# Rewriting a fused attention and Mish kernel: Mish as one ScalarE function from PSUM, k and q exponentials in the projection stage, attention combine beside the up-projection

## The chip, the core and the metric

The kernel runs on one core of one Trainium2 chip. The metric is the device time of one execution in microseconds (us); the profile's span of the same execution is about 2 us shorter. Before the change the median was 227.62 us over four runs (three of them 226.75 to 227.79, one slow at 241.48). Engines are named as the profile names them: PE is TensorE, PEld its weight loads, DVE VectorE, ACT ScalarE, POOL GpSimd, SP SyncE.

## The reference

Two branches read the same layer-normalised input of 2048 rows and 448 columns, and their results are added to the input.

```python
xn = _layernorm(x)                                  # x: (1, 2048, 448), bf16
# branch A: linear attention, 16 heads of 28 columns
q, k, v = split(xn @ wqkv)
pq, pk  = q @ w_phi, k @ w_phi                      # per head, 28 x 28
phi_q = concat([softmax(pq), softmax(-pq)])         # phi_k the same from pk
kv = einsum("bhsf,bhsd->bhfd", phi_k, v);  z = phi_k.sum(s)
o  = (phi_q @ kv) / (phi_q @ z + 1e-6)
A  = o.reshape(B, S, D) @ wo
# branch B: feed-forward, 448 -> 1792 -> 448, with Mish
h   = xn @ w1 + b1
B   = (h * tanh(log(1 + exp(h)))) @ w2             # written in a stable form there
return x + A + B
```

## The kernel before

Both kernels fold `w_phi` into the q and k weights first. The old kernel then computes Mish in three passes, with a change of ScalarE's function table between them. The parts that matter (cuts are marked `# ...`):

```python
# ScalarE and VectorE, up-projection: h has 56 groups of 512 columns, four PSUM banks in turn
for grp in range(NGRP):
    b_exp.inc(act.activation(sp_buf[:, fc, cols], hring[grp % HR], ACT.Exp, bias=b1T[:, fc:fc + 1]))
    # every fourth group on ScalarE, the others on VectorE: h + bias, kept in SBUF
    b_hb.inc(dve.tensor_scalar(hb_all[:, fc, cols], hring[grp % HR], b1T[:, fc:fc + 1], None, op0=ALU.add))
    # ... beside it k: two exponentials per tile on ScalarE, reduce and reciprocal on VectorE, phik on GpSimd

for fc in range(FC):                                             # second pass
    b_ln.inc(act.activation(sp_buf[:, fc, :], sp_buf[:, fc, :], ACT.Ln, bias=1.0))
# ... meanwhile TensorE does v and q, and VectorE copies q, unexponentiated, to SBUF

for k in range(2 * FC):                                          # third pass
    b_tanh.inc(act.activation(t_tmp[k % 2], sp_buf[:, fc, half], ACT.Tanh))
    b_mul.inc(dve.tensor_tensor(actT[:, fc, cols], hb_all[:, fc, cols], t_tmp[k % 2], ALU.mult))

# only then, per row tile: q exponentials, attention numerator and denominator, combine, output
for t in range(-2, NT):
    pe_nd(t + 2); pe_ffn2(t); pe_transposes(t + 1); pe_wo(t)     # TensorE
    # VectorE per tile: copy, two products, sum, reciprocal, product, and the residual
```

The softmax here doesn't subtract the row's maximum and nothing guards it: scores larger than these inputs give would overflow.

Of the kernel before, what the change touches and what calls it, by code (L numbers as in the profile page):

```python
# [6 lines left out]
ALU = mybir.AluOpType  # L7
# [4 lines left out]

# [7 lines left out]
KC = 4  # L20
KP = 112
FC = F // P
TCW = 512
TC = S // TCW
QG = 4
LN_EPS = 1e-5
NGRP = TC * FC
HR = 4
NDW = QG * (DH + 2)


class Ctr:

    def __init__(self, sem, name):
        self.sem = sem
        self.name = name
        self.n = 0

    def inc(self, ins, by=1, expect=None):
        ins.then_inc(self.sem, by)  # L40
        self.n += by
        if expect is not None:
            assert self.n == expect, f"{self.name}: count {self.n} != expected {expect}"
        return self.n


def wait(eng, ctr, val):
    if val > 0:
        assert val <= 30000, (ctr.name, val)
        eng.wait_ge(ctr.sem, val)  # L50
# [6 lines left out]
def bass_parallel_sum__linear_kernel_hedgehog__dense_activation_mish__prompt_kernel(  # L57
    nc, A_x, A_wqkv, A_w_phi, A_wo, B_x, B_w1, B_b1, B_w2, out
):
    es = ExitStack()  # L60
    with es:
        _kernel(es, nc, A_x, A_wqkv, A_w_phi, A_wo, B_w1, B_b1, B_w2, out)


def _kernel(es, nc, A_x, A_wqkv, A_w_phi, A_wo, B_w1, B_b1, B_w2, out):
    def C(name):
        return Ctr(es.enter_context(nc.semaphore(name)), name)

    def sb(name, shape, dtype, side, stack):
        return stack.enter_context(nc.sbuf_tensor(name, shape, dtype, side=side))  # L70

    x2 = A_x[0]
    out2 = out[0]

    PKGRP = [2 + round(i * (NGRP - 4) / (NT - 1)) for i in range(NT)]
    assert len(set(PKGRP)) == NT and PKGRP[-1] < NGRP

    L = es
    ident = sb("ident", [P, P], BF16, "left", L)
    eps_col = sb("eps_col", [P, 1], FP32, "left", L)  # L80
    Wbd = sb("Wbd", [KP, QG, KP], BF16, "left", L)
    b1_rows = sb("b1_rows", [FC, P], BF16, "left", L)
    b1T = sb("b1T", [P, FC], FP32, "left", L)
    KVZ1 = sb("KVZ1", [KP, 2 * QG, QG, DH + 2], BF16, "left", L)
    Wv = sb("Wv", [KP, KC, D], BF16, "left", L)
    Wpq = sb("Wpq", [KP, KC, D], BF16, "left", L)
    Wpk = sb("Wpk", [KP, KC, D], BF16, "left", L)
    xnT = sb("xnT", [KP, KC, S], BF16, "left", L)
    sL_A = ExitStack()
    x_all = sb("x_all", [P, NT, D], BF16, "left", sL_A)  # L90
    stats = [sb(f"stats{i}", [P, 6], FP32, "left", sL_A) for i in range(2)]
    mv = [sb(f"mv{i}", [P, 2], FP32, "left", sL_A) for i in range(2)]
    std = [sb(f"std{i}", [P, 1], FP32, "left", sL_A) for i in range(2)]
    rstd = [sb(f"rstd{i}", [P, 1], FP32, "left", sL_A) for i in range(2)]
    xn_buf = [sb(f"xn{i}", [P, D], BF16, "left", sL_A) for i in range(2)]
    peakA_left = nc.sbuf_base
    sL_A.close()
    hb_all = sb("hbact", [P, FC, S], BF16, "left", L)
    actT = hb_all
    t_tmp = [sb(f"t_tmp{i}", [P, TCW * 2], BF16, "left", L) for i in range(2)]  # L100
    sL_B = ExitStack()
    sp_buf = sb("sp_buf", [P, FC, S], BF16, "left", sL_B)

    sR_phik = ExitStack()
    phik = sb("phik", [P, NT, 2, D], BF16, "right", sR_phik)
    sR_W1 = ExitStack()
    W1 = sb("W1", [KP, KC, F], BF16, "right", sR_W1)
    sR_D1 = ExitStack()
    Ek = [sb(f"Ek{i}", [P, 2, D], BF16, "right", sR_D1) for i in range(2)]
    Sk = [sb(f"Sk{i}", [P, 2 * H], FP32, "right", sR_D1) for i in range(2)]  # L110
    rSk = [sb(f"rSk{i}", [P, 2 * H], FP32, "right", sR_D1) for i in range(2)]
    sR_A = ExitStack()
    Wqk_tmp = sb("Wqk_tmp", [KP, KC, 2 * D], BF16, "right", sR_A)
    WT_sb = [sb(f"WT_sb{i}", [KP, QG, KP], BF16, "right", sR_A) for i in range(2)]
    peakA = nc.sbuf_top - nc.sbuf_base
    sR_A.close()
    sR_D1.close()
    sR_W1.close()
    sR_C = ExitStack()
    v_ext = sb("v_ext", [P, NT, H, DH + 1], BF16, "right", sR_C)  # L120
    pqT_all = sb("pqT_all", [KP, QG, S], BF16, "right", sR_C)
    peakC = nc.sbuf_top - nc.sbuf_base
    sL_B.close()
    W2 = sb("W2", [P, FC, D], BF16, "left", L)
    Wo = sb("Wo", [KP, KC, D], BF16, "left", L)
    NEQ = 3
    NOSB = 3
    sR_E = ExitStack()
    es.enter_context(sR_E)
    EqT = [sb(f"EqT{i}", [KP, 2, QG, P], BF16, "left", sR_E) for i in range(NEQ)]  # L130
    t1 = [sb(f"t1_{i}", [P, H, DH + 1], FP32, "left", sR_E) for i in range(2)]
    t2 = [sb(f"t2_{i}", [P, H, DH + 1], FP32, "left", sR_E) for i in range(2)]
    rden = sb("rden", [P, H], FP32, "left", sR_E)
    Sq = [sb(f"Sq{i}", [P, 2, H], FP32, "left", sR_E) for i in range(2)]
    o_sb = [sb(f"o_sb{i}", [P, D], BF16, "left", sR_E) for i in range(NOSB)]
    oT_sb = [sb(f"oT_sb{i}", [KP, KC, P], BF16, "left", sR_E) for i in range(2)]
    out_sb = [sb(f"out_sb{i}", [P, D], BF16, "left", sR_E) for i in range(2)]
    x_ring2 = [sb(f"x_ring2_{i}", [P, D], BF16, "left", sR_E) for i in range(2)]
    peakE = nc.sbuf_top - nc.sbuf_base
    assert min(peakA, peakC, peakE) >= 0, (peakA, peakC, peakE)  # L140
    del peakA_left

    PB0 = es.enter_context(nc.psum_tensor("PB0", [P, TCW], FP32))
    PB1 = es.enter_context(nc.psum_tensor("PB1", [P, TCW], FP32))
    PBnd = es.enter_context(nc.psum_tensor("PBnd", [P, 2 * TCW], FP32))
    PB4 = es.enter_context(nc.psum_tensor("PB4", [P, TCW], FP32))
    PB5 = es.enter_context(nc.psum_tensor("PB5", [P, TCW], FP32))
    PB6 = es.enter_context(nc.psum_tensor("PB6", [P, TCW], FP32))
    PB7 = es.enter_context(nc.psum_tensor("PB7", [P, TCW], FP32))
    xT_ps = [PB0.bitcast(BF16)[:, 0:KC * P].rearrange("p (c n) -> p c n", c=KC),  # L150
             PB1.bitcast(BF16)[:, 0:KC * P].rearrange("p (c n) -> p c n", c=KC)]
    WT_ps = [PB6.bitcast(BF16)[:, 0:QG * KP].rearrange("p (g n) -> p g n", g=QG),
             PB5.bitcast(BF16)[:, 0:QG * KP].rearrange("p (g n) -> p g n", g=QG)]
    Wp_ps = [PB7[:, 0:D], PB4[:, 0:D]]
    b1T_ps = PB5.bitcast(BF16)[:, 1008:1024]
    hring = [PBnd[:, 0:TCW], PBnd[:, TCW:2 * TCW], PB4[:, :], PB5[:, :]]
    pk_ps = [PB6[:, 0:D], PB7[:, 0:D]]
    vring = [PB0[:, 0:D], PB1[:, 0:D]]
    kv_ps = [PBnd[:, 0:QG * (DH + 1)], PBnd[:, TCW:TCW + QG * (DH + 1)]]
    pqring = [PB4[:, :], PB5[:, :]]  # L160
    out_ps = [PB0[:, 0:D], PB1[:, 0:D], PB5[:, 0:D], PB6[:, 0:D], PB7[:, 0:D]]
    NOUT = len(out_ps)
    NEARLY = NOUT
    nd_ps = PBnd[:, :].rearrange("p (s n) -> p s n", s=2)
    oT_ps = PB4.bitcast(BF16)[:, 0:KC * P].rearrange("p (c n) -> p c n", c=KC)

    ld_x = [C(f"ld_x{i}") for i in range(4)]
    ld_w1 = C("ld_w1")
    ld_b1 = C("ld_b1")
    ld_wphi = C("ld_wphi")  # L170
    ld_wqk = C("ld_wqk")
    ld_wv = C("ld_wv")
    ld_w2a = C("ld_w2a")
    ld_w2b = C("ld_w2b")
    ld_wo = C("ld_wo")
    ld_x2 = [C("ld_x2_0"), C("ld_x2_1")]
    g_init = C("g_init")
    out_dma = [C("o_dma0"), C("o_dma1")]
    a_b1 = C("a_b1")
    a_dve = C("a_dve")  # L180
    a_st = C("a_st")
    a_ag = C("a_ag")
    a_sq = C("a_sq")
    a_rs = C("a_rs")
    a_xn = C("a_xn")
    a_tp = C("a_tp")
    a_cp = C("a_cp")
    a_wtp = C("a_wtp")
    a_wt = C("a_wt")
    a_wpm = C("a_wpm")  # L190
    a_wp = C("a_wp")
    b_pe = C("b_pe")
    b_hb = C("b_hb")
    b_hba = C("b_hba")
    b_exp = C("b_exp")
    d_pe = C("d_pe")
    d_exp = C("d_exp")
    d_red = C("d_red")
    d_rcp = C("d_rcp")
    d_phi = C("d_phi")  # L200
    b_ln = C("b_ln")
    b_tanh = C("b_tanh")
    b_mul = C("b_mul")
    c_pe = C("c_pe")
    c_dve = C("c_dve")
    c_pool = C("c_pool")
    e_pqa = C("e_pqa")
    c_pq = C("c_pq")
    d_kv = C("d_kv")
    d_kvz = C("d_kvz")  # L210
    d_fin = C("d_fin")
    e_expq = C("e_expq")
    e_nd = C("e_nd")
    e_ndrd = C("e_ndrd")
    e_dl = C("e_dl")
    e_o = C("e_o")
    e_tp = C("e_tp")
# [579 lines left out]
```

## Time and profile before

| stage of the old kernel | window, us | what limits it |
|---|---|---|
| layernorm, weight folding | 0 to 32 | a serial chain of VectorE and ScalarE |
| up-projection, k | 32 to 97 | TensorE |
| Ln pass, v, q | 97 to 124 | ScalarE |
| Tanh pass, kv | 124 to 154 | ScalarE |
| first combines | 154 to 178 | VectorE |
| down-projection | 178 to 225 | TensorE |

Lines of the profile page of the kernel before: the span; the busy time of each engine; and two rows in which the span is cut into 40 slices, PE's busy share and the clock granted to it, each in tenths (9 is 90% or more).

```profile
span 225.3 us, 3204 instructions
...
PE 186.9 (83%) x1153; PEld 105.6 (47%) x1153; DVE 166.2 (74%) x319; ACT 157.9 (70%) x244; POOL 41.8 (19%) x43
...
PE   0239869999999999959999862995576899999995
...
PEclk9999999999999999999999995899678599999999
```

PE is 83% busy, yet the digits dip between slices 23 and 32, and the clock dips with them.

The same kernel by stages: the window, then the busy time (and number of instructions) of PE, PEld, DVE, ACT and POOL, then the mean granted clock, the share of the DMA engines and GB/s.

```profile
0.00:32.00 32.00, 15.61 (x121) 13.05 (x121) 20.46 (x71) 15.62 (x38) 7.22 (x17) 1.00 0.55 147
32.00:97.00 65.00, 63.97 (x301) 29.94 (x302) 49.10 (x75) 59.52 (x106) 23.78 (x14) 1.00 0.00 1
97.00:124.00 27.00, 24.94 (x123) 13.87 (x123) 21.30 (x34) 26.97 (x17) 4.61 (x3) 1.00 0.00 1
124.00:154.00 30.00, 22.39 (x196) 13.70 (x193) 20.38 (x30) 29.48 (x38) 6.22 (x9) 0.89 0.25 68
154.00:178.00 24.00, 15.49 (x106) 8.96 (x107) 20.97 (x45) 12.71 (x24) 0.00 (x0) 0.75 0.15 43
178.00:225.30 47.30, 44.48 (x311) 26.07 (x310) 33.97 (x69) 13.55 (x25) 0.00 (x0) 0.98 0.20 57
```

In the third and fourth windows ACT is busy 27 of 27 and 29.5 of 30 us: the Ln and Tanh passes. In the fifth nothing but DVE is near full, PE works 15.5 of 24 us and its clock falls to 0.75. These 81 us are what the change goes after.

Groups of instructions: line, engine, operation, output and inputs, shapes, count, then busy time, mean duration in ns, idle time before.

```profile
L599 ACT ACTIVATE t_tmp<-sp_buf 128x1024 bf16<-128x1024 bf16 x28 | 27.7, 1053 | 0.0
L304 POOL TENSOR_TENSOR phik<-Ek,rSk 128x896 bf16<-128x896 bf16 x16 | 27.2, 1698 | 60.0 <-DVE rSk L681 59.8
...
L584 ACT ACTIVATE sp_buf<-sp_buf 128x2048 bf16<-128x2048 bf16 x14 | 25.3, 1895 | 0.0
...
L571 ACT ACTIVATE sp_buf<-PBnd,b1T 128x512 bf16<-128x512 f32 x28 | 19.0, 702 | 0.7 <-PE PBnd L389 0.4
```

The costs a prediction can start from: 0.70 us for a ScalarE function of 512 columns from PSUM with a bias, 25.3 and 27.7 us for the passes that go away, and 1.70 us for GpSimd's product of 896 columns.

### The profile page before, as it was taken

The numbers are of one execution on the slowest core, as the hardware profiler recorded it, in microseconds if no ns is written. First come the engines' busy times: TensorE is split into PE (matmuls) and PEld (weight loads), VectorE is DVE, ScalarE is ACT, GpSimd is POOL, SyncE is SP. The second block draws the span as 40 slices with busy tenths as digits, with TensorE's granted clock in tenths as the row PEclk, the third lists the DMA queues.
The fourth block names the chain that finished last, engine by engine and source line by source line (L and its number), as shares of the span: only waits on it lengthen the run. The fifth ranks groups of instructions, "written<-read, shape, count | busy, mean of one in ns | idle before, by whom it ended". The sixth has DMA issues, their size and how long they took to land.

```text
span 225.3 us, 3204 instructions
## 1 busy us (share of the span) xinstructions
PE 186.9 (83%) x1153; PEld 105.6 (47%) x1153; DVE 166.2 (74%) x319; ACT 157.9 (70%) x244; POOL 41.8 (19%) x43
## 2 busy tenths in 40 slices
PE   0239869999999999959999862995576899999995
PEld 0138744444444444425555751442443556566552
DVE  2539973578887878969878567775999997887831
ACT  2126876999999999899999999998355224335120
POOL 8220000053545344661000019000000000000000
PEclk9999999999999999999999995899678599999999
DMA  6968000000000000000000009301012221221211
GB/s 198 258 161 214 1 3 1 0 0 3 0 0 0 0 3 0 1 1 3 0 0 0 3 0 299 61 0 41 0 41 63 64 81 41 64 62 41 75 50 41
DMA packets 9710, 10.54 MB, mean 47 GB/s; under 512 B 832, under 2 KB 9232, under 8 KB 9696
## 3 DMA queue, kind: packets, MB, share of 16 engines
q1 hardware_dynamic: 9008, 7.51, 11.6%
q0 software_dynamic: 688, 2.84, 5.2%
q8 instruction: 9, 0.15, 0.3%
q14 instruction: 5, 0.04, 0.1%
HBM read 8.52 MB, written 1.84 MB: 46 GB/s over the span
## 4 chain that ended last, share of the span: by engine, by line
PE 50%; ACT 27%; DVE 13%; DMA 4%; issue 3%; POOL 2%; POOLq 0%; DVEq 0%; ACTq 0%
PE PB L484 13%; ACT t_tmp L599 11%; PE PBnd L389 11%; ACT sp_buf L584 11%; PE PB L389 11%; PE PB L371 5%; PE PB L503 4%; DMA Wqk_tmp<-in_A_wqkv_dram 4%; DVE stats L650 2%; PE PBnd L474 2%; PE PB L494 1%; POOL Wbd L289 1%; DVE WT_sb L658 1%; ACT std L526 1%; DVE o_sb L752 1%
## 5 line engine op out<-in xcount | busy, mean ns | idle before, releaser
L304 POOL TENSOR_TENSOR phik<-Ek,rSk 128x896 bf16<-128x896 bf16 x16 | 27.2, 1698 | 60.0 <-DVE rSk L681 59.8
L623 ACT ACTIVATE oT_sb<-PB 112x512 bf16<-112x512 bf16 x16 | 9.6, 598 | 38.3 <-PE PB L494 38.3
L484 PE MATMUL PB<-W,hbact 128*128 128x448 bf16 x154 | 31.4, 356 | 0.0
L695 DVE TENSOR_SCALAR hbact<-PBnd,b1T 128x512 bf16<-128x512 f32 x28 | 19.8, 727 | 14.5 <-ACT sp_buf L571 14.4
L389 PE MATMUL PBnd<-xnT,W 112*128 112x512 bf16 x112 | 28.6, 395 | 0.0
L599 ACT ACTIVATE t_tmp<-sp_buf 128x1024 bf16<-128x1024 bf16 x28 | 27.7, 1053 | 0.0
L389 PE MATMUL PB<-xnT,W 112*128 112x512 bf16 x112 | 27.1, 379 | 0.0
L725 DVE TENSOR_TENSOR hbact<-hbact,t_tmp 128x1024 bf16<-128x1024 bf16 x28 | 19.7, 703 | 9.4 <-ACT t_tmp L599 9.3
L584 ACT ACTIVATE sp_buf<-sp_buf 128x2048 bf16<-128x2048 bf16 x14 | 25.3, 1895 | 0.0
L571 ACT ACTIVATE sp_buf<-PB,b1T 128x512 bf16<-128x512 f32 x28 | 19.2, 694 | 3.2 <-PE PB L389 2.9
L462 PE MATMUL PB<-W,hbact 128*128 128x448 bf16 x70 | 15.1, 376 | 7.0 <-DMA W<-in_B_w_dram 6.0
L484 PEld LDWEIGHTS PB<-W,hbact 128*128 128x128 bf16 x154 | 14.9, 99 | 12.8 <-issue 0.4
L571 ACT ACTIVATE sp_buf<-PBnd,b1T 128x512 bf16<-128x512 f32 x28 | 19.0, 702 | 0.7 <-PE PBnd L389 0.4
L389 PEld LDWEIGHTS PBnd<-xnT,W 112*128 112x128 bf16 x112 | 11.3, 101 | 13.5 <-issue 1.7
L678 DVE TENSOR_REDUCE Sk<-Ek 128x32 f32<-128x896 bf16 x16 | 17.2, 1075 | 0.4 <-ACT Ek L557 0.4
L389 PEld LDWEIGHTS PB<-xnT,W 112*128 112x128 bf16 x112 | 11.0, 98 | 12.9 <-issue 0.3
L430 PE MATMUL PB<-xnT,Wpq 112*112 112x512 bf16 x64 | 16.4, 379 | 0.7 <-ACT hbact L574 0.7
L503 PE MATMUL PB<-Wo,oT_sb 112*128 112x448 bf16 x64 | 17.0, 394 | 0.0
L417 PE MATMUL PB<-Wv,xnT 112*128 112x448 bf16 x64 | 14.7, 353 | 2.1 <-DVE v_ext L708 2.1
L371 PE MATMUL PB<-Wpk,xnT 112*128 112x448 bf16 x64 | 14.7, 352 | 0.0
L474 PE MATMUL PBnd<-KVZ,EqT 112*128 112x120 bf16 x128 | 10.9, 238 | 4.0 <-DVE t_0 L743 2.4
L462 PEld LDWEIGHTS PB<-W,hbact 128*128 128x128 bf16 x70 | 7.0, 103 | 14.8 <-issue 7.9
(72 smaller groups left out, 306.3 us busy)
## 6 DMA issues: line engine op xcount, KB each, us to landing
x_all<-in_A_x_dram SPq DMA_DIRECT2D x4, 448.0 KB, 5.8
out_dram<-out_sb SPq DMA_DIRECT2D x16, 112.0 KB, 1.7
W<-in_B_w_dram POOLq DMA_DIRECT2D x1, 1568.0 KB, 8.8
W<-in_B_w_dram SPq DMA_DIRECT2D x2, 784.0 KB, 6.2
x_ring_0<-in_A_x_dram SPq DMA_DIRECT2D x8, 112.0 KB, 2.1
x_ring_1<-in_A_x_dram SPq DMA_DIRECT2D x8, 112.0 KB, 2.1
Wqk_tmp<-in_A_wqkv_dram POOLq DMA_DIRECT2D x1, 784.0 KB, 8.1
Wv<-in_A_wqkv_dram POOLq DMA_DIRECT2D x1, 392.0 KB, 9.3
```

Source lines behind the costliest of these rows:

```text
L304: d_phi.inc(gp.tensor_tensor(dst, src_, rs, ALU.mult), expect=t + 1)
L371: ins = pe.matmul(pk_ps[j], xnT[:, c, t * P:(t + 1) * P], Wpk[:, c, :], start=(c == 0), stop=(c == KC - 1))
L389: ins = pe.matmul(hring[grp % HR], W1[:, c, fc * P:(fc + 1) * P], xnT[:, c, tc * TCW:(tc + 1) * TCW], start=(c == 0), stop=(c == KC - 1))
L462: pe.matmul(out_ps[t % NOUT], actT[:, fc, t * P:(t + 1) * P], W2[:, fc, :], start=(fc == 0), stop=False)
L484: pe.matmul(out_ps[j], actT[:, fc, t * P:(t + 1) * P], W2[:, fc, :], start=(fc == 0), stop=False)
L503: ins = pe.matmul(out_ps[j], oT_sb[t % 2][:, c, :], Wo[:, c, :], start=False, stop=(c == KC - 1))
L571: b_exp.inc(act.activation(sp_buf[:, fc, tc * TCW:(tc + 1) * TCW], hring[grp % HR], ACT.Exp, bias=b1T[:, fc:fc + 1]), expect=grp + 1)
L584: b_ln.inc(act.activation(sp_buf[:, fc, :], sp_buf[:, fc, :], ACT.Ln, bias=1.0), expect=fc + 1)
L599: b_tanh.inc(act.activation(t_tmp[k % 2][:, :], sp_buf[:, fc, half * 1024:(half + 1) * 1024], ACT.Tanh), expect=k + 1)
L678: d_red.inc(dve.tensor_reduce(Sk[j][:, :], Ek[j][:, :, :].rearrange("p s (h f) -> p (s h) f", f=DH), AX.X, ALU.add), expect=t + 1)
L695: b_hb.inc(dve.tensor_scalar(hb_all[:, fc, tc * TCW:(tc + 1) * TCW], hring[grp % HR], b1T[:, fc:fc + 1], None, op0=ALU.add), expect=n_hb_d ...
L725: b_mul.inc(dve.tensor_tensor(actT[:, fc, cols], hb_all[:, fc, cols], t_tmp[k % 2][:, :], ALU.mult), expect=k + 1)
```

## The change

The intent: one ScalarE function (Mish) straight from PSUM in place of Exp, Ln and Tanh; the k and q exponentials straight from the projections' PSUM banks, before the up-projection; the attention combine hidden beside the up-projection's matmuls. The program is now recorded as a list of operations, from which the waits are derived. The diff rewrites nearly every line, so it is cut here to its core; names follow the new kernel.

```diff
-    b_ln.inc(act.activation(sp_buf[:, fc, :], sp_buf[:, fc, :], ACT.Ln, bias=1.0))
-    b_tanh.inc(act.activation(t_tmp[k % 2][:, :], sp_buf[:, fc, ...], ACT.Tanh))
-    b_mul.inc(dve.tensor_tensor(actT[:, fc, cols], hb_all[:, fc, cols], t_tmp[k % 2][:, :], ALU.mult))
+    # up-projection group n: 1024 columns, two banks
+    act(lambda a: a.activation(hm[tcp][:, fc, :], PS[:, b:b + 2, :], ACT.Mish, bias=b1T[:, fc:fc + 1]), ...)
 ...
-    a_sq.inc(act.activation(std[j][:, :], mv[j][:, 1:2], ACT.Sqrt, bias=eps_col[:]))
-    a_rs.inc(dve.reciprocal(rstd[j][:, :], std[j][:, :]))
-    a_xn.inc(dve.tensor_scalar(xn_buf[j], x_all[:, t, :], mv[j][:, 0:1], rstd[j], op0=ALU.subtract, op1=ALU.mult))
+    def ln_rstd(t, n):                       # 1/std on GpSimd: add eps, then power -0.5
+        pool(lambda g: g.tensor_scalar(rstd[:, t:t + n], ..., LN_EPS, None, op0=ALU.add), ...)
+        pool(lambda g: g.tensor_tensor(rstd[:, t:t + n], rstd[:, t:t + n], mhalf[:, 0:n], ALU.pow), ...)
+    def ln_norm(t, eng):
+        eng(lambda v: v.tensor_scalar(xn[t % NXN], x_all[:, t, :], mv[:, t, 0:1], rstd[:, t:t + 1],
+                                      op0=ALU.subtract, op1=ALU.mult), ...)
 ...
+    def kexp(j):                             # a pair of row tiles; Ek has two buffers
+        for s in range(2):
+            act(lambda a, s=s: a.activation(Ek[j % 2][:, :, s, :], PS[:, 4:6, 0:D], ACT.Exp,
+                                            scale=(1.0 if s == 0 else -1.0)), ...)
+    def knorm(j):
+        b = j % 2
+        dve(lambda v: v.tensor_reduce(Sk[b], Ek[b], AX.X, ALU.add), ...)
+        dve(lambda v: v.reciprocal(rSk[b], Sk[b]), ...)
+        pool(lambda g: g.tensor_tensor(phik[:, 2 * j:2 * j + 2, :], Ek[b], rSk[b] (broadcast), ALU.mult), ...)
 ...
+    ln(0, dve); ...; ln(1, dve); ln(2, pool)
+    for j in range(NP):                      # eight pairs of row tiles
+        vproj(j)
+        kproj(j); kexp(j)
+        if j + 1 < NP: xT(j + 1)             # x transposes and their copy to SBUF
+        if j >= 1: qproj(...); qexp(...)
+        if j + 3 < NP: ln(j + 3, pool)       # normalisation on GpSimd
+        if j == 2: masks()                   # on GpSimd
+        if j >= 1: knorm(j - 1)
+    qproj(3, 1); qexp(3, 1); knorm(NP - 1)
+    for n in range(2 * FC):                  # up-projection
+        ffn1(n)
+        if n == 5: kvz()
+        if 0 <= n - 6 < NT: nd(n - 6)        # attention and combine of one row tile
+        if 0 <= n - 9 < NT: oTr(n - 9)
+    for t in range(NT): final(t)             # down- and output projection, residual
```

## The prediction

> **What bounds it now.** Span 225.3 us (227.79 timed). The chain of waits is 50% TensorE, 27% ScalarE, 13% VectorE; the limit changes by stage (engine busy time by windows, timeline):
> - 0-32 us, layernorm and weight folding: a serial VectorE/ScalarE chain of 1.2-1.5 us per row tile.
> - 32-97: up-projection and k, TensorE (64.0 of 65 busy).
> - 97-124: the Ln pass on ScalarE (14 x 1.9 us), v and q matmuls beside it.
> - 124-154: the Tanh pass on ScalarE (29.5 of 30).
> - 154-178: attention combine, a VectorE chain near 3.3 us per tile; TensorE 15.5 of 24, clock 0.75.
> - 178-225: down-projection, TensorE: 3.6-4.05 us per tile, of which 14x0.19+4x0.19 = 3.4 is matmul.
>
> **Necessary TensorE work at full clock**, from spacing in the trace (512 columns 0.216 us, 448 columns 0.19, 120 columns 0.073, kv 0.056): up-projection 48.4, q 13.8, v and k 24.3, kv 7.2, combine 9.3, down 42.6, output projection 12.2, transposes 10-15: about 170 us. Some 55 us are waits and cold clock.
>
> **What changes.** Removed: Exp on h (28+28 x 0.70 us), Identity, bias adds on VectorE (42 x 0.72), Ln 25.3, Tanh 27.7, product 19.7, q evacuation 11.0, sixteen Sqrt. Added: 28 Mish of 1024 columns from PSUM. [...] One table load (1.28 us) between Exp and Mish. Combine shrinks to about 2.0 us of VectorE per tile, beside matmuls.
>
> **Sum of the new stages** (estimates):
> 1. Head, to the first dense projection: 12-13 us (weight folding waits for GpSimd's small loads).
> 2. Projections, eight pairs of tiles. Work per pair: TensorE 5.5, VectorE 5.3 (reduce 2.0, reciprocal 0.55, v copy 1.1, statistics 1.5), GpSimd 5.5-6 (phik 3.4, from 1.70 at half size), ScalarE 4.5. Not the work but a cycle binds: k exponential 1.7 -> x transpose copy 1.0 -> v matmuls 1.6 -> v copy 1.2 -> statistics 1.5 -> reduce/reciprocal 2.6 -> phik 3.5 -> k exponential two pairs later: 13.1, so 6.6 us per pair while statistics run, 5.8 after. First pair 9. Ends near 67.
> 3. Up-projection with kv and combine: 48.4+7.2+16x0.93 = 70.5, TensorE-bound; the two combine banks are freed about 2.1 us after they fill, just what TensorE needs to return: 1-2 us of stalls. Ends near 139.
> 4. Down-projection 16 x 3.42 = 54.7: ends near 194; tail 2.8.
>
> Span 195-197; **time 197 us**, 8 in 10 between **187 and 208**. Faster by over 2%: 0.97; within 2%: 0.02; slower: 0.01. About 54 us of Ln and Tanh passes and 20 us of combine stage leave the critical path; about 40 us of that return as TensorE work moved beside them or projections slower than pure matmul time.
>
> **Right if:** two table loads; Mish near 1.13 us each, spaced 1.9-2.8 us by TensorE; up-projection stage 71-75 us at TensorE above 93% busy, clock near 1; down-projection tiles near 3.45 us; projection pairs near 6.6 then 5.8 us with the k exponential waiting for GpSimd.
>
> **Wrong if:** [...]GpSimd's normalisation or power is slow, so projection pairs take 8 us (+12); the projection stage leaves the clock low (+5 to 10); combine banks stall TensorE 1 us per group (+16); or projections run at TensorE's 5.5 us (-8).

The sum came to: the head and the projections to 67 us, the up-projection to 139, the down-projection to 194, the tail 2.8, together 195 to 197 us of span. No term of it is cut: in the stage with Mish it counts TensorE's matmuls alone. What is cut is the working of Mish's 1.13 us, which did not come from a trace, and one clause under "Wrong if". An estimate from the trace of the kernel before comes to nearly the same: 0.70 us for 512 columns from PSUM (L571), plus 512 more at 0.82 ns each (1.053 us for 1024 columns, L599, and 1.895 for 2048, L584), is 1.12 us, under the 1.73 us that a group's eight matmuls take (L389).

## The result, and the profile after

The median was **212.08 us** (210.47 to 212.95, four runs). The ratio to the kernel before is 0.9335, with a 95% interval of 0.9276 to 0.9394. The change is faster, as forecast, but by 15 us instead of 31; the time lies above the range of 187 to 208.

The same lines of the page for the kernel after, with GpSimd's row added:

```profile
span 210.4 us, 2756 instructions
...
PE 181.3 (86%) x1153; PEld 98.0 (47%) x1153; DVE 83.3 (40%) x160; ACT 84.5 (40%) x94; POOL 76.6 (36%) x70
...
PE   0587689395894896899999999999999999999994
...
POOL 8366449999996329200033333442000000000000
PEclk9999699887899797999999999999999999999999
```

The dip has moved. It is now deepest between slices 8 and 16, and POOL's row shows 9 from slice 7 to slice 12.

By stages:

```profile
0.00:23.70 23.70, 11.76 (x96) 8.61 (x97) 7.70 (x21) 10.93 (x12) 15.55 (x25) 0.99 0.98 267
23.70:85.70 62.00, 48.86 (x236) 24.79 (x235) 32.63 (x40) 33.23 (x37) 45.94 (x29) 0.87 0.03 7
85.70:153.00 67.30, 66.20 (x539) 36.70 (x537) 32.98 (x83) 39.20 (x45) 15.09 (x16) 1.00 0.01 1
153.00:210.40 57.40, 54.54 (x288) 27.96 (x286) 10.00 (x16) 1.11 (x1) 0.00 (x0) 1.00 0.10 33
```

The border at 85.7 us is the start of the table load before the first Mish. TensorE's first up-projection matmul starts earlier, at 83.55, and its first down-projection matmul at 152.81. So the last two stages went as predicted or better: the up-projection with all combines inside it took 67.3 us from the table load, or 69.3 from its first matmul (predicted 71 to 72), and the down-projection and tail 57.4 us (54.7 + 2.8). Everything before the first up-projection matmul takes 83.55 us where the prediction had 67. In the second window PE works 48.9 of 62 us at a clock of 0.87, and no engine is full: POOL, the busiest after PE, shows 45.9.

Groups of the kernel after:

```profile
L430 ACT ACTIVATE hm<-PS,b1T 128x1024 bf16<-128x1024 f32 x28 | 31.2, 1114 | 28.2 <-PE PS L420 28.1
L338 POOL TENSOR_TENSOR hm<-hm,rSk 128x1792 bf16<-128x1792 bf16 x8 | 25.7, 3217 | 9.3 <-DVE rSk L337 9.2
L263 POOL TENSOR_SCALAR xn<-x_all,mv,rstd 128x448 bf16<-128x448 bf16 x12 | 22.3, 1867 | 0.6
...
L263 DVE TENSOR_SCALAR xn<-x_all,mv,rstd 128x448 bf16<-128x448 bf16 x4 | 1.4, 393 | 2.3 <-POOL rstd L259 2.3
```

Mish takes 1.114 us; the estimate was 1.13. But the last two lines are the same operation, same shape, on two engines: 0.39 us on DVE, **1.87 us on POOL**. The prediction had put about 0.85 us per tile into its 5.5 to 6 us of GpSimd work: half of the 1.70 us that the product of 896 columns took in the old kernel.

One pair in the timeline (start, duration, engine, line, operation; in brackets the engine's idle time just before and what ended it):

```profile
47.20 0.24 POOL L257 TENSOR_SCALAR rstd<-mv 128x2 f32<-128x2 f32 x1
47.27 1.73 ACT L330 ACTIVATE hm<-PS 128x896 bf16<-128x896 f32 x2 [5.48 <-POOL hm L338]
...
47.52 0.72 POOL L259 TENSOR_TENSOR rstd<-rstd,mhalf 128x2 f32<-128x2 f32 x1
48.35 3.72 POOL L263 TENSOR_SCALAR xn<-x_all,mv,rstd 128x448 bf16<-128x448 bf16 x2
48.88 1.03 ACT L301 ACTIVATE xnT<-PS 112x1024 bf16<-112x1024 bf16 x1
...
49.97 2.79 PE L310 MATMUL PS<-Wqkv,xnT 112*128 112x448 bf16 x8 [2.88 <-ACT xnT L301]
...
52.04 3.21 POOL L338 TENSOR_TENSOR hm<-hm,rSk 128x1792 bf16<-128x1792 bf16 x1
...
55.26 0.23 POOL L257 TENSOR_SCALAR rstd<-mv 128x2 f32<-128x2 f32 x1
55.28 0.92 ACT L330 ACTIVATE hm<-PS 128x896 bf16<-128x896 f32 x1 [3.54 <-POOL hm L338]
```

POOL does not pause: 1/std, two normalisations, phik, then the next 1/std at 55.26, 8.06 us after the one at 47.20. The k exponentials (ACT L330) wait each time until a phik has ended, 5.48 and 3.54 us. The x transposes' copy (L301) is next in ScalarE's order, and TensorE's v matmuls (L310) wait for it, 2.88 us of doing nothing after which the clock has dropped (0.58 granted between 49.9 and 52.8 us; 2.79 us for eight matmuls that take 1.69 at 31.01, where the clock was 1.00).

### The profile page after: what moved, and what is told of

It is laid out like the page before. It is cut to its first block, busy times and chain, and to the rows that moved or that the text cites. A ratio compares the mean times of both kernels' runs of the same rounds, so it can differ in the third digit from the quotient of the medians.

```text
span 210.4 us, 2756 instructions
## 1 busy us (share of the span) xinstructions
PE 181.3 (86%) x1153; PEld 98.0 (47%) x1153; DVE 83.3 (40%) x160; ACT 84.5 (40%) x94; POOL 76.6 (36%) x70
## 4 chain that ended last, share of the span: by engine, by line
PE 65%; POOL 17%; ACT 9%; DVE 4%; DMA 3%; issue 1%; ACTq 0%; POOLq 0%; DVEq 0%
PE PS L439 20%; PE PS L420 19%; POOL xn L263 7%; POOL hm L338 6%; PE PS L444 6%; PE PS L310 4%; PE PS L384 4%; ACT hm L330 3%; PE PS L365 3%; PE PS L323 3%; DMA Wbd<-in_A_w_phi_dram 3%; ACT EqT L356 2%; PE PS L406 2%; PE PS L349 2%; POOL rstd L259 1%; PE PS L284 1%
## 5 line engine op out<-in xcount | busy, mean ns | idle before, releaser
L420 PE MATMUL PS<-xnT,W 112*128 112x512 bf16 x224 | 52.5, 381 | 0.6 <-ACT hm L430 0.6
L439 PE MATMUL PS<-W,hm 128*128 128x448 bf16 x224 | 45.0, 353 | 0.0
L430 ACT ACTIVATE hm<-PS,b1T 128x1024 bf16<-128x1024 f32 x28 | 31.2, 1114 | 28.2 <-PE PS L420 28.1
L420 PEld LDWEIGHTS PS<-xnT,W 112*128 112x128 bf16 x224 | 21.0, 98 | 23.3 <-ACT hm L430 1.4
L449 DVE TENSOR_TENSOR out_sb<-PS,x_all 128x448 bf16<-128x448 f32 x16 | 10.0, 625 | 54.5 <-PE PS L444 54.5
L439 PEld LDWEIGHTS PS<-W,hm 128*128 128x128 bf16 x224 | 21.9, 98 | 20.6
L338 POOL TENSOR_TENSOR hm<-hm,rSk 128x1792 bf16<-128x1792 bf16 x8 | 25.7, 3217 | 9.3 <-DVE rSk L337 9.2
L310 PE MATMUL PS<-Wqkv,xnT 112*128 112x448 bf16 x64 | 19.0, 457 | 11.1 <-ACT xnT L301 11.1
L330 ACT ACTIVATE hm<-PS 128x896 bf16<-128x896 f32 x16 | 13.8, 914 | 26.3 <-POOL hm L338 17.1
L263 POOL TENSOR_SCALAR xn<-x_all,mv,rstd 128x448 bf16<-128x448 bf16 x12 | 22.3, 1867 | 0.6
L349 PE MATMUL PS<-xnT,Wp 112*112 112x512 bf16 x64 | 16.4, 402 | 2.0 <-ACT EqT L356 2.0
L310 PEld LDWEIGHTS PS<-Wqkv,xnT 112*128 112x128 bf16 x64 | 7.0, 119 | 20.7 <-ACT xnT L301 13.5
L323 PE MATMUL PS<-Wp,xnT 112*128 112x448 bf16 x64 | 15.9, 399 | 0.6 <-ACT hm L277 0.6
L335 DVE TENSOR_REDUCE Sk<-hm 128x64 f32<-128x1792 bf16 x8 | 16.0, 1995 | 0.0
L323 PEld LDWEIGHTS PS<-Wp,xnT 112*128 112x128 bf16 x64 | 6.9, 111 | 8.7 <-issue 3.7
L251 DVE BATCH_NORM_STATS2 stats<-x_all 128x6 f32<-128x448 bf16 x16 | 9.2, 614 | 4.3 <-DMA x_all<-in_A_x_dram 4.3
```

The costliest lines, as they stand in the source:

```text
L263: eng(lambda v: v.tensor_scalar(xn[t % NXN][:, :], x_all[:, t, :], mv[:, t, 0:1], rstd[:, t:t + 1], op0=ALU.subtract, op1=ALU.mult), r=[f" ...
L310: i = e.matmul(PS[:, 2 + u, 0:D], xnT[:, c, t * P:(t + 1) * P], Wqkv[:, c, 2 * D:3 * D], start=(c == 0), stop=(c == KC - 1))
L323: i = e.matmul(PS[:, 4 + u, 0:D], xnT[:, c, t * P:(t + 1) * P], Wp[:, 1, c, :], start=(c == 0), stop=(c == KC - 1))
L330: act(lambda a, s=s: a.activation(Ek[j % 2][:, :, s, :], PS[:, 4:6, 0:D], ACT.Exp, scale=(1.0 if s == 0 else -1.0)), w=[f"Ek{j % 2}{s}"], ...
L335: dve(lambda v: v.tensor_reduce(Sk[b][:, :], Ek[b][:, :, :, :].rearrange("p t s (h f) -> p (t s h) f", f=DH), AX.X, ALU.add), r=[f"Ek{b}0" ...
L338: pool(lambda g: g.tensor_tensor(phik[:, 2 * j:2 * j + 2, :].rearrange("p t (k f) -> p (t k) f", f=DH), Ek[b][:, :, :, :].rearrange("p t s ...
```

## The experiments

The theories at the start: **A**, GpSimd's own 7.9 us of work per pair, one instruction after the other, is the limit; **B**, the cycle through the two buffers of k exponentials (exponential, reduction, phik, and back to the exponential two pairs later) is. All kernels below are the kernel after with the edit shown, unless said otherwise. The medians quoted are over all runs; for the kernel before and for runs 2 and 7 they include one slow run, which moves them by less than 0.2 us. Results are correct unless a wrong one is announced. Runs 1 to 4 were made on one chip and runs 5 to 12 on another, so small differences between runs are read from the ratios, each taken to the old kernel on the same chip. "Pairs" are the distances between successive k exponentials in the trace. The first of them says little: it is 8.8 us in the kernel after and 7.2 in run 11, where nothing before it was changed; run 5 has 7.2 as well. In the profile of the kernel after the granted clock between 23 and 27 us was 0.57.

### 1. Normalise on VectorE

```diff
-    ln(2, pool)
+    ln(2, dve)
-            ln(j + 3, pool)
+            ln(j + 3, dve)
```

> Edit: the twelve row-tile normalisations of pairs 2 to 7 run on VectorE (0.39 us each there in the trace of the changed kernel) instead of GpSimd (1.87 us each). Theory A, GpSimd's own work (1/std 0.95 + two normalisations 3.72 + phik 3.2 = 7.9 us per pair, in order) sets the pace of the projection stage: the first Mish starts near 70 us instead of 85.7, pairs near 6.6 us or less, granted clock in the stage rises, time 195 to 199 us, ratio to before about 0.865. Rival B, the cycle through the two buffers of k exponentials sets it whatever GpSimd's normalisation costs: under 4 us gained, time 208 to 212.

Measured: 208.86 us, ratio 0.9158 (0.9091 to 0.9225). First Mish at 83.6. Only 3 to 4 us gained, as B had said, but the reason was a third one. One pair of this run in the timeline:

```profile
44.26 0.22 POOL L257 TENSOR_SCALAR rstd<-mv 128x2 f32<-128x2 f32 x1
...
44.57 0.72 POOL L259 TENSOR_TENSOR rstd<-rstd,mhalf 128x2 f32<-128x2 f32 x1
45.32 0.70 DVE L263 TENSOR_SCALAR xn<-x_all,mv,rstd 128x448 bf16<-128x448 bf16 x2 [1.81 <-POOL rstd L259]
...
45.94 2.01 DVE L335 TENSOR_REDUCE Sk<-hm 128x64 f32<-128x1792 bf16 x1
...
47.98 0.55 DVE L337 RECIPROCAL rSk<-Sk 128x64 f32<-128x64 f32 x1
...
48.61 3.21 POOL L338 TENSOR_TENSOR hm<-hm,rSk 128x1792 bf16<-128x1792 bf16 x1 [3.33 <-DVE rSk L337]
...
51.79 0.22 POOL L257 TENSOR_SCALAR rstd<-mv 128x2 f32<-128x2 f32 x1
```

Pairs take 7.5 us, and the chain is closed by two engines waiting for each other. VectorE's normalisation (L263) waits 1.81 us for 1/std, which sits on GpSimd behind the previous phik; the k reduction (L335) stands behind the normalisation in VectorE's order; the next phik waits for it; and the next 1/std, at 51.79, waits for that phik. Moving the work took 3.7 us per pair off GpSimd and put a wait on VectorE into the ring. So this run does not decide between A and B.

### 2. Four buffers of k exponentials

```diff
-    Ek = [... for i in range(2)]        # and Ek[j % 2] in kexp and knorm
+    Ek = [... for i in range(4)]        # and Ek[j % 4]; the space was free
```

> Edit: four buffers of k exponentials instead of two, normalisation left on GpSimd. Theory A (GpSimd's in-order work of 7.9 us per pair): little gained, 0 to 5 us, time 207 to 212, GpSimd still over 90% busy between 25 and 65 us; the waits move from the k exponential to the x transposes that wait for normalised tiles. Rival B (the cycle through the two buffers): 10 us or more gained, time under 202.

Measured: 199.57 us, ratio 0.8772 (0.8730 to 0.8814): 12 to 13 us gained with GpSimd's work unchanged. Theory A in its simple form falls. (The profiled run was slow, at 202.63 us; pairs of nearly the same length, 5.93 us, appear in run 3's fast profile.) Two k exponentials of this run:

```profile
40.06 1.73 ACT L330 ACTIVATE hm<-PS 128x896 bf16<-128x896 f32 x2 [1.46 <-PE PS L323]
...
46.06 1.73 ACT L330 ACTIVATE hm<-PS 128x896 bf16<-128x896 f32 x2 [1.53 <-PE PS L323]
```

They are 6.00 us apart (five of this run's pairs are 5.9 to 6.0 us, the last 8.9), and wait for the k matmuls (L323), no longer for GpSimd. GpSimd starts a 1/std at 29.1, 37.2, 47.1 and 55.1 us, against 29.3, 37.3, 47.2 and 55.3 in the kernel after: as slow as before. Its backlog is worked off later, five phik in a row after 59.9 us, where only the kv matmuls need them. So GpSimd's slowness cost time because two buffers handed it on to ScalarE and from there to TensorE.

### 3. Both

> Edit: both together. If the buffer cycle of the prediction (6.6 us per pair) binds once GpSimd is relieved, this gains 4 to 8 us more than the first run alone: pairs near TensorE's 5.5 or VectorE's 6.0 us, time 190 to 194. If it does not bind, time equals the first run's within 2 us.

Measured: 202.18 us, ratio 0.8898 (0.8863 to 0.8934): better than run 1, as expected, but short of the 190 to 194, and slower than run 2 alone. Some pairs are 5.93 us apart, but GpSimd's 1/std still stands behind phik, so VectorE still waits for it (12.0 us in all, the head included), its reductions keep a pace of 7.5, and VectorE's copies of v fall behind. One late pair is 9.2 us long: in it the v matmuls start only after such a copy, and take 3.02 us (57.67) where the next pair's take 1.69. Here, with four buffers, taking a slow operation off an engine that no longer limited anything only harmed the one that received it.

### 4. What GpSimd's normalisation costs by itself

Wrong results on purpose; one look. The normalisation of each pair of tiles is written in another way:

```diff
+        if t // 2 == 3: eng(tensor_scalar(o, a, rstd[:, t:t + 1], None, op0=ALU.mult))
+        if t // 2 == 4: eng(tensor_scalar(o, a, 0.01, 20.0, op0=ALU.subtract, op1=ALU.mult))
+        if t // 2 == 5: eng(tensor_scalar(o, a, 20.0, None, op0=ALU.mult))
+        if t // 2 == 6: eng(tensor_tensor(o, a, rstd (broadcast), ALU.mult))
+        if t // 2 == 7: eng(tensor_copy(o, a))
```

> Wrong result on purpose, one look: the GpSimd instruction that writes the normalised tile is replaced, a pair of tiles each, by: multiply by a per-partition scalar only (pair 3), subtract and multiply by constants (pair 4), multiply by a constant (pair 5), a two-tensor multiply by 1/std broadcast (pair 6), a copy (pair 7); pair 2 is unchanged at 1.87 us. If the cost is in the two arithmetic steps, one-step forms take about half; if it is in the per-partition scalars, the constant forms are much shorter than 1.87; if it is GpSimd's rate per element for any input, all are alike. From phik (3.2 us for 1792 elements) the two-tensor form should take 0.9 us, so less than the one-input form it replaces.

The POOL groups (L280 unchanged, L269 two constants, L266 one per-partition scalar, L272 one constant, L275 two tensors, L278 copy):

```profile
L280 POOL TENSOR_SCALAR xn<-x_all,mv,rstd 128x448 bf16<-128x448 bf16 x2 | 3.7, 1858 | 0.1
L269 POOL TENSOR_SCALAR xn<-x_all 128x448 bf16<-128x448 bf16 x2 | 3.4, 1717 | 0.2
L266 POOL TENSOR_SCALAR xn<-x_all,rstd 128x448 bf16<-128x448 bf16 x2 | 2.8, 1405 | 0.1
L272 POOL TENSOR_SCALAR xn<-x_all 128x448 bf16<-128x448 bf16 x2 | 2.7, 1336 | 0.1
...
L275 POOL TENSOR_TENSOR xn<-x_all,rstd 128x448 bf16<-128x448 bf16 x2 | 1.8, 932 | 0.1
...
L278 POOL COPY xn<-x_all 128x448 bf16<-128x448 bf16 x2 | 1.1, 553 | 0.1
```

None of the three readings fits alone. A one-step form still takes 1.34 to 1.41, so it is not mainly the number of steps (the second adds 0.38 to 0.45 us); constants in place of pointers save 0.07 to 0.14. It is the operation: a `tensor_scalar` of one input is slower here than a product of two tensors, 0.93 us, close to the rate of phik (2.1 against 1.8 ns per column). A copy takes 0.55. The time of this kernel, 205.37 us, is a single run whose state is unknown, so only the durations are used.

### 5. GpSimd as the prediction had assumed it

Wrong result: each GpSimd normalisation becomes one two-tensor product, 0.93 us (1.82 for the two of a pair).

```diff
     def ln_norm(t, eng):
+        if eng is pool:
+            pool(lambda g: g.tensor_tensor(xn[t % NXN], x_all[:, t, :], rstd (broadcast), ALU.mult), ...)
+            return
```

> Wrong result on purpose: in the changed kernel the twelve normalisations on GpSimd are each replaced by one two-tensor multiply on GpSimd, measured at 0.93 us in the probe, close to the 0.85 us or so that the prediction had put in. Nothing else changes, two buffers of k exponentials. If the mis-sized normalisation is what stretched the buffer cycle, pairs fall from 8.0 to about 6.6 us (the one with the masks to about 8.5) and the time to 201 to 204 us. If the cycle is set by something else, the time stays above 209.

Measured: 204.16 us, ratio 0.8995 (0.8944 to 0.9045), inside the expected 201 to 204 but for 0.2 us. Against the kernel after this is 0.034 of 227 us, or about 8 us: roughly half of the miss of 15 is this one term. Pairs after the first: 7.1, 8.0, 7.7, then 6.0 three times. The predicted 6.6 was not met in the early ones; the pair of 8.0 contains GpSimd's masks, and the one of 7.7 a wait of TensorE of 2.62 us and slower matmuls after it (eight of v 2.37 us and eight of k 2.73, against 1.69 and 1.68 in the next pair).

### 6 and 7. Normalise on VectorE, after the k reduction

The wait of run 1 can be ordered away: statistics and 1/std early, then `knorm(j - 1)`, then the normalisation. Run 6 has two buffers of k exponentials, run 7 four.

```diff
-    ln(2, pool)
+    ln(2, dve)
 ...
         if j + 3 < NP:
-            ln(j + 3, pool)
+            ln(j + 3, None)                  # statistics and 1/std only
         ...
         if j >= 1:
             knorm(j - 1)
+        if j + 3 < NP:
+            for t in (2 * j + 6, 2 * j + 7):
+                ln_norm(t, dve)
```

> Normalisation on VectorE as in the first run, but issued after the k reduction, so that VectorE no longer waits for 1/std behind phik. Two buffers. If the first run's 7.5 us per pair came from that wait (phik 3.2 + 1/std 1.2 + normalise 0.6 + reduce 1.9 + reciprocal 0.6), pairs fall to about 6.4, the buffer cycle of the prediction, and the time to 199 to 203 us. If two buffers alone give 7.5 us, nothing changes: 207 to 209.

> The same with four buffers of k exponentials. The buffer cycle is gone; what remains in the trace of the second run is a cycle of 5.93 us through ScalarE and TensorE (two k exponentials 1.73, transpose copy 0.91, v matmuls 1.69, k matmuls 1.53), and VectorE's own 6.0 us. Pairs near 6.0 from the second to the last, first Mish near 74, time 195 to 198 us. If GpSimd still matters it is as in the third run: 202.

Measured: run 6 209.89 us, ratio 0.9240 (0.9181 to 0.9298); run 7 206.75 us, ratio 0.9102 (0.9044 to 0.9159). Both miss by 7 to 12 us; run 7 is even slower than run 3. The suspect is one line of run 7's timeline, here with the GpSimd line that goes with it and TensorE's next v matmuls:

```profile
48.75 3.51 DVE L263 TENSOR_SCALAR xn<-x_all,mv,rstd 128x448 bf16<-128x448 bf16 x2
48.91 3.21 POOL L339 TENSOR_TENSOR hm<-hm,rSk 128x1792 bf16<-128x1792 bf16 x1 [1.46 <-DVE rSk L338]
...
53.40 2.68 PE L310 MATMUL PS<-Wqkv,xnT 112*128 112x448 bf16 x8 [2.83 <-DVE v_ext L314]
```

The two normalisations, 0.70 us in runs 1 and 3, take 3.51 us here. They begin 0.16 us before phik and end 0.14 us after it; of the two, one took 0.30 us and the other 3.29. In the new order VectorE issues them right after the reciprocal, which is also what releases phik, so they meet it in all four pairs of the loop that have both, in run 6 too (3.5 us three times and 4.2 once, behind the masks). VectorE's copy of v comes behind them, and in two pairs of run 7 TensorE's v matmuls wait 2.85 and 2.83 us for it.

Not every VectorE instruction is slowed like this: k reductions keep their 2.0 us beside phik, in the kernel after for example (2.01 us at 60.70, beside the phik at 60.08). So the guess was that this form of the normalisation is slow while phik runs. Run 9 puts it to the test.

### 8. A first combination

Run 7, with in addition: the x transposes and their copy ahead of the k matmuls; statistics and 1/std of pairs 4 to 7 and the whole layernorm of pair 3 taken early, and each normalisation issued one pair sooner; masks after the loop; the small weight loads issued from ScalarE's queue; the second half of the k folding in other banks.

> The previous kernel, with in addition: the x transposes and their copy before the k matmuls and exponentials (breaks the 5.93 us cycle), all statistics and 1/std of pairs 4 to 7 taken in VectorE's idle head, masks built after the projections, small weight loads issued from ScalarE's queue instead of GpSimd's, and the second half of the k folding in other banks. Pairs near TensorE's 5.3 to 5.5 us, first Mish near 66 to 69, time 188 to 192 us. If TensorE is not what is left, over 194.

Measured: 196.06 us, ratio 0.8657 (0.8610 to 0.8704), 4 us above the expected range. Undisturbed pairs are 5.2 to 5.3 us apart, but three pairs still hold a 3.51 us normalisation beside phik (the first at 29.06 us), and one of these pairs took 9.1 us.

### 9. Is it this form of the instruction?

Run 7 with one change: the normalisation also writes an accumulator that nobody reads.

```diff
                                       op0=ALU.subtract, op1=ALU.mult
-                                      ), ...)
+                                      , accum_out=acc[:, t:t + 1]), ...)
```

> The seventh kernel (normalise on VectorE after the k reduction, four buffers; 206.75 us), with one change: the normalisation also writes an accumulator, which nobody reads (the result may be wrong, which does not matter here). [...] If that is why two normalisations took 3.51 us beside phik, they take about 1.2 us here (0.6 each[...]), pairs fall to about 6 us and the time to 196 to 200 us. If they were waiting for something else, 3.5 us stays and the time is 206 or more.

What is cut is the reason given for the expectation, which no run shows. "That" stands for the guess above: the normalisation in the form of run 7 is slow beside phik, and the accumulating form need not be. The 0.6 us each is an estimate; other VectorE operations on 448 columns took 0.61 and 0.63 us in the kernel after (statistics L251, residual L449).

Measured: 198.58 us, ratio 0.8769 (0.8693 to 0.8844), inside the expected range and 8 us faster than run 7. The result was wrong (relative error 0.45). The place in the timeline that corresponds to the one above:

```profile
46.28 0.64 DVE L264 TENSOR_SCALAR_CACHE_REDUCE xn<-x_all,mv,rstd 128x448 bf16<-128x448 bf16 x1
46.44 3.21 POOL L340 TENSOR_TENSOR hm<-hm,rSk 128x1792 bf16<-128x1792 bf16 x1 [1.46 <-DVE rSk L339]
...
46.85 0.73 DVE L264 TENSOR_SCALAR_CACHE_REDUCE xn<-x_all,mv,rstd 128x448 bf16<-128x448 bf16 x1
```

Slower by itself (0.64 and 0.73 instead of 0.39 us), the pair of instructions now runs beside phik and is done in 1.3 us. Pairs are 5.93 us from the second to the sixth. No operation was moved and no wait for a result was removed, so the 3.51 us were not spent waiting for another engine's result: they belong to this form of the instruction running beside phik. Why that form is slowed was not shown.

### 10. Everything of layernorm before the first phik

From the kernel after, one thing: all statistics, 1/std and normalisations are taken in VectorE's idle head (its first 25 us; in the kernel after it is busy 7.70 us of the first 23.70), the results of the later tiles in space that is unused until Mish writes it.

```diff
-    ln(1, dve)
-    ln(2, pool)
+    # statistics, 1/std (still GpSimd) and normalisation (VectorE) of all pairs, interleaved
+    ln_a(2, 4); ln_a(4, 6); ln_b(2, 4); ln_a(6, 8); ln_b(4, 6); ln_a(8, 16); ln_b(6, 8)
 ...
-        if j + 3 < NP:
-            ln(j + 3, pool)
+        if j == 0:
+            ln_b(8, 16)
```

> From the changed kernel, one thing: all statistics, 1/std and normalisations are taken before GpSimd's first phik, in VectorE's idle head, normalisations on VectorE. Two buffers of k exponentials, masks where they were. GpSimd has only phik (3.2 us) and the masks left in the loop, and no normalisation can overlap it. Theory now: the loop was a ring through the two buffers, stretched by whatever GpSimd does besides phik. Then the ring is 1.73+0.95+1.6+1.1+2.6+3.3 = 11.3 us per two pairs = 5.65, below the 5.93 us cycle of ScalarE and TensorE, so pairs of 5.93, one longer for the masks; time 196 to 199 us. If GpSimd's load in the loop is not what matters, 205 or more.

Measured: 201.46 us, ratio 0.8873 (0.8810 to 0.8936): 10 to 11 us gained with two buffers, 2.5 us above the expected range. Five of the six pairs are 5.99 us apart, so two buffers are enough once GpSimd has only phik in the loop. The remaining pair took 8.24. The masks were done by 35.5 us and did not hold it up: VectorE waited 2.71 us for a small transpose of the bias that stands behind pair 2's projections in TensorE's order, the k reduction waited behind it, and so did the phik for which the next k exponential waited 3.77 us.

### 11. The q tail

From the kernel after, one thing: the last q projection uses the two banks of the x transposes instead of waiting for the exponentials of the one before.

```diff
+        qb = 0 if (tc, gp) == (3, 1) else 6       # in qproj and qexp, for banks 6 and 7
-        b = 2 * (n % 2)                           # in ffn1
+        b = 2 * ((n + 1) % 2)
```

> From the changed kernel, one thing: the last q projection goes to the two banks that the x transposes used, so it need not wait for the exponentials of the one before, and the up-projection starts with the other bank pair. The last k exponential to the first Mish took 10.1 us in the changed kernel, of which 2.0 us wait and 3.2 us cold matmuls between the q exponentials; this removes 3 to 4 us: time 208 to 209.5 us. If the tail is bound elsewhere, 211 or more.

Measured: 209.04 us, ratio 0.9231 (0.9161 to 0.9301), 2 to 3 us gained: inside the expected range, though the two intervals of the ratio overlap a little (0.9276 to 0.9394 for the kernel after). The last k exponential to the first Mish went from 10.1 to 6.7 us.

### 12. A second combination

Run 8's other edits, run 10's layernorm and run 11's tail.

> The combined kernel again, with normalisations in the head so that none meets phik, and the q tail of the other run: four buffers, transposes before k, masks late, small weight loads from ScalarE's queue, k folding in other banks. Pairs 5.2 to 5.3 us throughout, no cold clock in the loop, first Mish near 64 to 67 us, time 189 to 192 us; over 194 would mean that something else than these waits is left.

Measured: **189.63 us** (189.53 to 190.37, four runs), ratio 0.8368 (0.8316 to 0.8420) to the kernel before; correct, and inside the expected range. It beats both kernels. The first three stages:

```profile
0.00:25.00 25.00, 14.98 (x114) 10.41 (x115) 17.18 (x51) 12.02 (x14) 7.69 (x19) 0.93 0.97 267
25.00:64.40 39.40, 38.99 (x223) 22.09 (x222) 26.41 (x24) 34.52 (x38) 23.94 (x8) 1.00 0.01 2
64.40:133.00 68.60, 67.52 (x547) 37.59 (x546) 32.98 (x83) 38.97 (x44) 18.87 (x22) 1.00 0.00 1
```

Between 25 us and the first Mish, TensorE is busy 39.0 of 39.4 us at full clock; pairs from the second on are at most 5.4 us apart, as run 8's undisturbed ones were. These windows are cut at the first Mish and not at the up-projection's matmuls; from its first matmul to the first of the down-projection that stage takes 69.3 us, as in the kernel after. How the gain splits between the edits of this run was not measured one by one.

## Why the prediction was wrong

The direction was right, and so was most of the sum. Point by point:

- **Mish as one ScalarE pass: right.** 28 of 1.114 us, predicted 1.13. Two table loads, 1.28 us each, as predicted.
- **Up-projection, TensorE-bound, with the combine hidden: right, and better.** 67.3 us from the table load, or 69.3 from its first matmul, instead of 71 to 72; 98% busy and at full clock. A group with combine and transposes takes 2.50 us where 2.66 was assumed, and the two combine banks stalled TensorE only for the first few tiles.
- **Down-projection: right.** 3.41 us per tile; 54.6 us, predicted 54.7.
- **"Projections, eight pairs of tiles": wrong.** Predicted to end near 67 us, they ended at 83.55, where the up-projection's matmuls begin. The term that was mis-sized is "GpSimd 5.5-6 (phik 3.4 ...)": phik was 3.2, but the two normalisations took 3.7 us, not about 1.7, so that with 1/std GpSimd had 7.9 us of work per pair. With it fell the sentence "Not the work but a cycle binds". The cycle that the prediction lists has only phik of GpSimd in it and takes 6.6 us per pair; GpSimd's queue, 1/std and normalisations before each phik, took longer, and from 29.3 to 63.3 us GpSimd did not pause: pairs took 9.01, 9.94 (with the masks), 8.01 and 8.05 us. The predicted link between the engines was right: the k exponential waited for the phik of two pairs before. It needs both, the long queue and the two buffers. Four buffers with the same queue gain 12 to 13 us (run 2), and two buffers with a shorter queue gain 8 (run 5) or 10 to 11 (run 10). I had taken the rate of a two-input product in the trace as an upper bound for a one-input operation on the same engine; run 4 shows the opposite order, 0.93 against 1.86. Run 5, with nearly the assumed cost, gives 204.2: about 8 of the 15 us.
- **What the sum left out.** The chain from the last k exponential to the first Mish takes 10.1 us, and I had let the up-projection start when the last q projection ends; run 11 took 2 to 3 us of this back. The pair with the masks took 9.9 us; GpSimd's 2 us of masks were not in the sum. The first pair ended at 23.7 us instead of 21 to 22. And after waits of TensorE of 3.5 and 2.9 us the granted clock was 0.52 and 0.58 over the next 3 us (0.87 in that stage as a whole), which the prediction had listed only under its risks. These together are more than the other 7 us, since the up-projection gave back about 3; except for run 11 they were not measured apart, so how those 7 us divide stays open.
- **"Wrong if": named, and not weighed.** The prediction says that slow GpSimd normalisation would make pairs 8 us long and add 12 us. That is what happened, and an upper end of 208 did not hold it (197 + 12 is 209).

Two steps of my own theories fell on the way. That GpSimd's work alone, whatever the buffers, was the limit fell with run 2. That moving the normalisation to the engine that does it in 0.39 us would bring the gain fell with runs 1, 3, 6 and 7: in runs 1 and 3 because 1/std stood behind phik in GpSimd's order (a wait of 1.81 us in the pair shown), in runs 6 and 7 because two normalisations beside phik took 3.51 us instead of 0.70.

## What to carry to other kernels

When an engine looks like the limit, ask who passes its lateness on: here a two-deep buffer did, and two more buffers were worth more (12 to 13 us) than giving the slow work to an engine that does it in a fifth of the time (3 to 4 us). Before moving an operation, look at what stands before and after it in the new engine's order, and measure it beside what will run next to it: two normalisations took 0.70 us alone and 3.51 beside phik. In run 10, work done in VectorE's idle head met no phik at all. And cost an operation by its own form on its own engine: a duration of a neighbouring form in the trace is no bound.

## What else the traces showed

- On GpSimd, bf16, 128 x 448, a one-input `tensor_scalar` took 1.34 us (one constant) to 1.86 us (two per-partition scalars), against 0.93 us for the two-input product and 0.55 us for a copy (run 4); VectorE's two-scalar form took 0.39 (kernel after). So of these one-input forms only the copy was faster than the two-input product.
- An operation released by the same event as a GpSimd instruction met it every time: four pairs of four in runs 6 and 7, 3.50 to 4.17 us for the two normalisations, against 1.3 us in the accumulating form of run 9.
- A low clock followed shorter waits of TensorE, too: in the kernel after, one of 2.0 us before the last q projection was followed by a mean clock of 0.60 over the next 3.1 us, and eight 512-column matmuls took 3.18 us instead of 1.89. Nor does the length of the wait decide alone: in run 7, eight v matmuls took 1.67 us after a wait of 2.85 us and 2.68 us after one of 2.83.
- The power operation on GpSimd took 0.72 us for two columns (kernel after) and 1.66 us for eight (run 8).
